# Linear attention and a gated MoE block on one core: MoE chunks of 384 tokens, queries in token order, and TensorE's order fixed as traced

## The chip, the core and the metric

The kernel runs on one core of one Trainium2 chip. The metric is device time in microseconds (us), as the median of several runs. The engines are TensorE (PE; its weight loads are listed as PEld), VectorE (DVE), ScalarE (ACT), GpSimd (POOL) and SyncE (SP), which issues all the DMAs of data here.

## The reference

```python
def _attn_ref(q, k, v, w_phi):                  # q, k, v: 8 batches, 8 heads, 576 tokens, 64
    def phi(x):
        proj = np.einsum('bhsd,df->bhsf', x, w_phi)               # 128 features
        proj = proj - np.max(np.abs(proj), axis=-1, keepdims=True)
        return np.concatenate([np.exp(proj), np.exp(-proj)], axis=-1)
    q_p, k_p = (phi(q), phi(k))
    kv = np.einsum('bhsf,bhsd->bhfd', k_p, v)
    z = np.sum(k_p, axis=2)
    num = np.einsum('bhsf,bhfd->bhsd', q_p, kv)
    den = np.einsum('bhsf,bhf->bhs', q_p, z)[..., None] + 1e-06
    return num / den

def _moe_ref(x, w_in, conv_w, w_out):           # x: 8 x 576 x 512, the heads side by side
    h = np.maximum(x @ w_in, 0.0)               # 1024 wide
    conv_out = sum over k of conv_w[k] * h shifted by k - 1 tokens    # zeros outside a batch
    gate = 1.0 / (1.0 + np.exp(-conv_out))
    return h * gate @ w_out                     # 512 wide
```

## The kernel before

**Attention.** The eight heads of a batch go as two quads (`qd`), and a quad's tokens as five groups (`g`): group 0 is the last 64 tokens of two head pairs, groups 1 to 4 are 256 columns each, two pieces (`t`) of 128 tokens for two heads (`i`). For a group of keys `k_process` loads it, splits it on GpSimd into a high and a low part (`kxh`, `kxl`), multiplies by the feature weights on TensorE in three matmuls a piece (`kp`, L194 to L196), takes the largest absolute value on VectorE (`km`, L199), subtracts it (`ks`, L201), forms both exponentials on ScalarE (`ke`, L223 and L224) and accumulates the product with `v`, which carries a column of ones, in PSUM (`kv`, L236 and L240). When a quad's five groups are done, ScalarE copies the sums out (`kvf`). For a group of queries `q_process` does the same up to `qs`, transposes on TensorE (`tp`, L280), exponentiates (`qe`), multiplies by `kvf` (`nm`, L297) and divides on VectorE (`dn`, `rc`, `x`). Queries of batch 0 are projected without the split, in F32 (L191). `x_process` transposes the result back (`xt`, `xr`) and splits it into `xh` and `xl`, one pair of tiles for a quad of a batch.

**MoE.** A batch's 576 tokens go as two chunks of `TC = 288`, each with one or two columns of its neighbour, 290 in all. `h_part(n)` makes eight tiles of hidden features with 12 matmuls each (`hp`, L356: high by high, low by high, high by low, over four pieces of the 512 inputs), and ScalarE applies the ReLU (`h`). `conv_process(n)` takes the middle tap on GpSimd and the outer taps on VectorE (`c`, L384), one sigmoid over the whole chunk on ScalarE (L388), the gate's product on VectorE (L392) and the split into `gh` and `gl`. `o_part(n)` makes four output tiles with 24 matmuls each (`op`, L415), which ScalarE copies (`os`) and SP writes out. The order is `h_part(n)`, then `o_part(n - 1)`.

**Weights.** `w_in` and `w_out` come as 64-bit floats in 16 tiles. For each, `float64_round` runs four VectorE instructions on a tile `w_t` (L91, L93, L95, L98), two on ScalarE (L92, L97) and one on GpSimd (L100); ScalarE and GpSimd then split it. Two buffers each hold the raw and the rounded tile.

**What sets the order.** All of this is written as generators. A loop at the end (`step`, `runnable`) keeps its own clock `now`, and picks the next step of attention or of the MoE so that the shares left of both shrink alike. A step ends with a cost, for instance `yield pe(450)` for the four (in the trace eight) instructions of a product piece, or with a wait:

```python
        yield pe(330 * n)
        yield wait(3000)
        yield until(back("kv", 1))
```

Chains are begun in the order of the list `chains`: a group of queries, then a group of the next quad's keys. The instructions are then ordered on each engine by a scheduler that plays them through with its own costs; a step runs under `tc.high_priority(offset=...)`, so that attention goes ahead of the MoE there.

Of the kernel before, what the change touches and what calls it, by code (L numbers as in the profile page):

```python
# [20 lines left out]
TC = 288  # L21
HW = TC + 2
VW = D + 1
NH = 11

WINDOW = 13
LAT = 1.7
TAIL_US = 24
AHEAD = 300

NQ_F32 = 2


@with_exitstack
def kernel(
# [108 lines left out]

    now = [0.0]
    ready = {}

    def pe(ns):
        return ("pe", ns)
# [17 lines left out]
    def load_split(src, b, qd, g, kind):  # L167
        c0, n = group_columns(g)
        if kind == "q" and 2 * b + qd < NQ_F32:
            raw = sb.tile([P, n * P], F32, name=f"{kind}r{b}_{qd}_{g}", tag=kind + "xh", bufs=2)  # L170
            nc.sync.dma_start(out=raw, in_=src[b, qd, :, c0 : c0 + n * P])
            return n, raw, None
        raw = sb.tile([P, n * P], F32, name=f"{kind}r{b}_{qd}_{g}", tag=kind + "r", bufs=2)
        nc.sync.dma_start(out=raw, in_=src[b, qd, :, c0 : c0 + n * P])
        hi = sb.tile([P, n * P], F32R, name=f"{kind}xh{b}_{qd}_{g}", tag=kind + "xh", bufs=2)
        lo = sb.tile([P, n * P], F32R, name=f"{kind}xl{b}_{qd}_{g}", tag=kind + "xl", bufs=2)
        split(raw, hi, lo, nc.gpsimd, nc.gpsimd)
        return n, hi, lo

    def project(n, hi, lo, b, qd, g, kind):  # L180
# [6 lines left out]
        for t in range(n):  # L187
            o = ps[:, t * 256 : (t + 1) * 256]
            his = hi[:, t * P : (t + 1) * P]
            if lo is None:  # L190
                nc.tensor.matmul(out=o, lhsT=his, rhs=wbd_f, start=True, stop=True)  # L191
                continue
# [3 lines left out]
            nc.tensor.matmul(out=o, lhsT=los, rhs=wbd_hi, start=False, stop=True)  # L196
        ps3 = ps.rearrange("p (t f) -> p t f", f=F)
        m = sb.tile([P, 2 * n], F32, name=f"{kind}m{b}_{qd}_{g}", tag="m", bufs=4)
        nc.vector.tensor_reduce(out=m, in_=ps3, axis=AX, op=ALU.max, apply_absolute_value=True)  # L199
        pr = sb.tile([P, 2 * n, F], F32, name=f"{kind}s{b}_{qd}_{g}", tag=kind + "s", bufs=2)  # L200
        nc.vector.tensor_tensor(out=pr, in0=ps3, in1=m.unsqueeze(2).broadcast_to([P, 2 * n, F]), op=ALU.subtract)  # L201
# [5 lines left out]
    def k_process(b, qd, g):  # L207
# [4 lines left out]

        yield until(back("kp", 2), back("kv", 4))
        n, hi, lo = load_split(kT, b, qd, g, "k")
        v0 = 16 if g == 0 else 4 * (g - 1)
        v = sb.tile([P, 4 * VW], F32, name=f"v{b}_{qd}_{g}", tag="v", bufs=4)
        nc.sync.dma_start(out=v, in_=vt[b, qd, :, v0 * VW : (v0 + 4) * VW])
# [3 lines left out]
        pr = project(n, hi, lo, b, qd, g, "k")  # L221
        e = sb.tile([P, 2, 2 * n, F], F32, name=f"ke{b}_{qd}_{g}", tag="ke", bufs=2)
        nc.scalar.activation(out=e[:, 0], in_=pr, func=AF.Exp)  # L223
        nc.scalar.activation(out=e[:, 1], in_=pr, func=AF.Exp, scale=-1.0)  # L224
        yield pe(330 * n)
# [5 lines left out]
        for t in range(n):  # L231
            for i in range(2):
                for s in range(2):
                    lhsT = e[:, s, 2 * t + i, :]
                    if g == 0:
                        nc.tensor.matmul(out=kp[i][:, s, :], lhsT=lhsT, rhs=v[:, 2 * i * VW : 2 * (i + 1) * VW],  # L236
                                         start=(s == 0), stop=False, skip_group_check=True)
                    else:
# [4 lines left out]
            yield pe(900 if g == 0 else 450)  # L243
        if g == 4:

            u = 2 * b + qd
            yield until(("num", u - 2, 4) if u > 1 else None)
            r = []
            for i in range(2):
                kf = sb.tile([P, 2, 2 * VW], F32, name=f"kvf{b}_{qd}_{i}", tag="kvf", bufs=4)  # L250
                nc.scalar.activation(out=kf, in_=kp[i], func=AF.Copy)
                r.append(kf)
            kv[b, qd] = r
            set_ready(("kvq", b, qd), 1500)
# [5 lines left out]
    def q_process(b, qd, g):  # L260
        j = (b * NQ + qd) * 5 + g

        def back(key, k):
            return (key, *divmod(j - k, 5)) if j >= k else None

        yield until(back("qp", 2))
        n, hi, lo = load_split(qT, b, qd, g, "q")
        yield wait(3000)
        yield until(back("tp", 2))
        set_ready(("qp", *divmod(j, 5)))  # L270
        pr = project(n, hi, lo, b, qd, g, "q")
        yield pe(330 * n)
        yield wait(1700)
        yield until(back("num", 2))
        set_ready(("tp", *divmod(j, 5)))
# [5 lines left out]
        qe = sb.tile([P, 2, 2, n, P], F32, name=f"qe{b}_{qd}_{g}", tag="qe", bufs=2)  # L281
        for s in range(2):
            nc.scalar.activation(out=qe[:, s], in_=tp, func=AF.Exp, scale=1.0 - 2.0 * s)  # L283
        yield pe(220 * n)
        yield wait(2000)
        yield until(back("num", 1), ("kvq", b, qd))
        if b > 1:
            yield until(("xt", b - 2, qd))
# [5 lines left out]
        for t in range(n):  # L294
# [5 lines left out]
            yield pe(900 if g == 0 else 450)  # L300
        dn = sb.tile([P, n, 2], F32, name=f"dn{b}_{qd}_{g}", tag="dn", bufs=4)
        rc = sb.tile([P, n, 2], F32, name=f"rc{b}_{qd}_{g}", tag="rc", bufs=4)
        x = sb.tile([P, n, 2, D], F32, name=f"x{b}_{qd}_{g}", tag="x0" if g == 0 else "x", bufs=2 if g == 0 else 4)
        xs[b, qd, g] = x
        parts = [(0, 64, 0), (64, 128, VW)] if g == 0 else [(0, P, 0)]
        for a, z, c0 in parts:
            nc.vector.tensor_scalar(out=dn[a:z], in0=ps[a:z, :, :, c0 + D], scalar1=1e-6, scalar2=None, op0=ALU.add)
        nc.vector.reciprocal(out=rc, in_=dn)
        for a, z, c0 in parts:
            nc.vector.tensor_tensor(out=x[a:z], in0=ps[a:z, :, :, c0 : c0 + D],  # L310
                                    in1=rc[a:z].unsqueeze(3).broadcast_to([z - a, n, 2, D]), op=ALU.mult)
        set_ready(("num", *divmod(j, 5)))
        if g == 2 or g == 4:
            spawn(x_process(b, qd, g // 2 - 1))

    def x_process(b, qd, pr):

        yield ("wait", 2500)
        if pr == 0:

            yield until(("h", 2 * (b - 2) + 1) if b > 1 else None)
            xh[b, qd] = sb.tile([P, 2, S], F32R, name=f"xh{b}_{qd}", tag="xh", bufs=4)
            xl[b, qd] = sb.tile([P, 2, S], F32R, name=f"xl{b}_{qd}", tag="xl", bufs=4)
        hi, lo = xh[b, qd], xl[b, qd]
        with tc.high_priority():
            xt = pg.tile([P, 4, P], F32, name=f"xt{b}_{qd}_{pr}", tag="g", bufs=4)
            for t in range(4):
                nc.tensor.transpose(out=xt[:, t, :], in_=xs[b, qd, 1 + 2 * pr + t // 2][:, t % 2], identity=idn)  # L328
            split(xt.rearrange("p t s -> p (t s)"), hi[:, pr, : 4 * P], lo[:, pr, : 4 * P], nc.scalar, nc.vector)
            if pr == 0:  # L330
                xr = pg.tile([P, 2, 64], F32, name=f"xr{b}_{qd}", tag="g", bufs=4)
                nc.tensor.transpose(out=xr, in_=xs[b, qd, 0][:, 0], identity=idn)
                split(xr, hi[:, :, 4 * P :], lo[:, :, 4 * P :], nc.scalar, nc.vector)
        set_ready(("x", b, 2 * qd + pr), 2500)
        if pr == 1:
            set_ready(("xt", b, qd))
        yield pe(550)
# [6 lines left out]
    def h_part(n):  # L344
        b, c = divmod(n, 2)
# [139 lines left out]
    while moe is not None or chains or active:  # L485
# [16 lines left out]
        if can_a and (a_first or not can_m):  # L502
# [3 lines left out]
            if not more:  # L506
                active.remove(p)
# [62 lines left out]
```

## Time and profile before

| | us |
|---|---|
| median of 3 runs | 867.71 |
| lowest and highest | 866.76, 872.09 |
| the profiled execution | 865.62 |
| its span, first to last instruction | 863.8 |

A busy time is the time in which an engine has at least one instruction running. Matmuls overlap: the next one starts while the last one drains, so the duration of one (about 300 ns for the MoE's) says less than the distance between two. The chain of waits, followed back from the last instruction, gives that distance, as it counts for each instruction only what it adds to the chain. Names are those of the program, without the buffer's number: `nm<-kvf,qe` writes `nm` and reads `kvf` and `qe`.

### The profile page before, as it was taken

Reading aid. Unit: us, or ns where it says so; the run is one execution under the profiler, and the core shown is the slowest. Engines: PE = TensorE matmul, PEld = TensorE weight load, DVE = VectorE, ACT = ScalarE, POOL = GpSimd, SP = SyncE. Lnnn points to the kernel's source line nnn. Section 1 sums busy time; section 2 is a strip of 40 time slices with the busy share of each in tenths; the row PEclk is TensorE's granted clock in tenths of the full one; section 3 lists DMA queues with packets and bytes.
Section 4 is the critical chain, followed back from the end, with each engine's and each line's share of the span. In section 5 each row is a group of like instructions: output and inputs, shape, how many; then the busy total and the mean of one; then the engine's idle time right before and its main releaser. Section 6 shows DMA issues by size and latency. Waiting matters only on the chain.

```text
span 863.8 us, 17401 instructions
## 1 busy us (share of the span) xinstructions
PE 832.9 (96%) x6654; PEld 823.9 (95%) x6654; DVE 554.4 (64%) x1222; ACT 401.3 (46%) x812; POOL 279.0 (32%) x466
## 2 busy tenths in 40 slices
PE   7888899999999999999999999999999999999998
PEld 6878899999999998999989999899999999999998
DVE  5999967866657556575566656666566756655461
ACT  4666634745354534435344444444454444433332
POOL 4766844323314132241323314232232412201110
PEclk9998999999999999999999999999999999999999
DMA  6544311112111111211112011211111100000001
GB/s 184 176 144 135 106 49 56 41 37 62 39 58 51 40 44 38 64 45 48 38 52 69 27 53 37 60 56 32 52 50 59 54 27 28 1 28 29 22 14 49
DMA packets 46594, 48.70 MB, mean 56 GB/s; under 512 B 5296, under 2 KB 44464, under 8 KB 46512
## 3 DMA queue, kind: packets, MB, share of 16 engines
q1 hardware_dynamic: 46512, 47.59, 18.3%
q8 instruction: 53, 0.87, 0.4%
q14 instruction: 29, 0.24, 0.1%
HBM read 38.13 MB, written 9.44 MB: 55 GB/s over the span
## 4 chain that ended last, share of the span: by engine, by line
PE 79%; DVE 12%; ACT 4%; issue 2%; DMA 1%; POOL 1%; SPq 0%; ACTq 0%; POOLq 0%; DVEq 0%
PE hp L356 23%; PE op L415 20%; PE nm L297 11%; PE kv L240 9%; PE tp L280 3%; DVE c L392 3%; PE kp L194 2%; PE kp L196 2%; PE qp L194 2%; PE kp L195 2%; PE qp L196 2%; PE qp L195 2%; DVE ks L201 1%; PE xt L328 1%; ACT c L388 1%
## 5 line engine op out<-in xcount | busy, mean ns | idle before, releaser
L384 DVE SCALAR_TENSOR_TENSOR c<-h,cw,c 128x288 f32<-128x288 f32 (+1 forms) x256 | 135.8, 537 | 84.1 <-POOL c L379 80.6
L297 PE MATMUL nm<-kvf,qe 128*128 128x65 f32 (+1 forms) x1152 | 162.7, 268 | 2.5 <-DVE ks L201 1.3
L356 PE MATMUL hp<-xh,win_hi 128*128 128x290 f32 x512 | 155.5, 305 | 0.9 <-ACT os L420 0.7
L297 PEld LDWEIGHTS nm<-kvf,qe 128*128 128x128 f32 x1152 | 152.6, 193 | 3.2 <-issue 1.5
L415 PE MATMUL op<-gh,wout_hi 128*128 128x288 f32 x512 | 154.9, 303 | 0.0
L356 PE MATMUL hp<-xh,win_lo 128*128 128x290 f32 x512 | 154.1, 301 | 0.0
L356 PE MATMUL hp<-xl,win_hi 128*128 128x290 f32 x512 | 153.7, 300 | 0.0
L415 PE MATMUL op<-gl,wout_hi 128*128 128x288 f32 x512 | 153.4, 300 | 0.0
L415 PE MATMUL op<-gh,wout_lo 128*128 128x288 f32 x512 | 152.4, 298 | 0.0
L240 PE MATMUL kv<-v,ke 128*128 128x65 f32 x1024 | 139.8, 267 | 4.6 <-ACT ke L223 4.6
L379 POOL TENSOR_SCALAR c<-h,cw 128x288 f32<-128x288 f32 x128 | 67.1, 525 | 234.7 <-ACT h L363 221.7
L240 PEld LDWEIGHTS kv<-v,ke 128*128 128x128 f32 x1024 | 133.7, 193 | 6.1 <-ACT ke L223 5.9
L363 ACT ACTIVATE h<-hp 128x290 f32<-128x290 f32 x128 | 52.8, 413 | 172.0 <-PE hp L356 164.5
L283 ACT ACTIVATE qe<-tp 128x512 f32<-128x512 f32 (+1 forms) x160 | 79.0, 554 | 49.1 <-PE tp L280 45.1
L356 PEld LDWEIGHTS hp<-xh,win_hi 128*128 128x128 f32 x512 | 96.8, 190 | 1.8 <-ACT os L420 1.4
L356 PEld LDWEIGHTS hp<-xl,win_hi 128*128 128x128 f32 x512 | 97.3, 190 | 0.0
L356 PEld LDWEIGHTS hp<-xh,win_lo 128*128 128x128 f32 x512 | 97.2, 190 | 0.0
L415 PEld LDWEIGHTS op<-gh,wout_lo 128*128 128x128 f32 x512 | 96.4, 188 | 0.0
L415 PEld LDWEIGHTS op<-gl,wout_hi 128*128 128x128 f32 x512 | 96.3, 188 | 0.0
L415 PEld LDWEIGHTS op<-gh,wout_hi 128*128 128x128 f32 x512 | 96.2, 188 | 0.0
L61 POOL TENSOR_SCALAR kxh<-kr 128x256 fp32r<-128x256 f32 (+1 forms) x80 | 33.8, 424 | 192.8 <-PE kp L195 167.8
L392 DVE TENSOR_TENSOR c<-c,h 128x288 f32<-128x288 f32 x128 | 58.4, 526 | 32.7 <-ACT c L388 32.7
(71 smaller groups left out, 1491.2 us busy)
## 6 DMA issues: line engine op xcount, KB each, us to landing
v<-in_vt_dram SPq DMA_DIRECT2D x80, 130.0 KB, 2.1
out_dram<-os SPq DMA_DIRECT2D x64, 144.0 KB, 1.7
qr<-in_qT_dram SPq DMA_DIRECT2D x64, 128.0 KB, 2.1
kr<-in_kT_dram SPq DMA_DIRECT2D x64, 128.0 KB, 2.1
w_r<-in_w_in_dram SPq DMA_DIRECT2D x8, 512.0 KB, 3.4
w_r<-in_w_out_dram SPq DMA_DIRECT2D x8, 512.0 KB, 3.3
qr<-in_qT_dram SPq DMA_DIRECT2D x16, 64.0 KB, 1.9
kr<-in_kT_dram SPq DMA_DIRECT2D x16, 64.0 KB, 2.0
```

The lines of the kernel that those rows point to most:

```text
L194: nc.tensor.matmul(out=o, lhsT=his, rhs=wbd_hi, start=True, stop=False)
L195: nc.tensor.matmul(out=o, lhsT=his, rhs=wbd_lo, start=False, stop=False)
L196: nc.tensor.matmul(out=o, lhsT=los, rhs=wbd_hi, start=False, stop=True)
L240: nc.tensor.matmul(out=kp[i][:, s, p0 : p0 + VW], lhsT=lhsT, rhs=v[:, (2 * t + i) * VW : (2 * t + i + 1) * VW], start=False, stop=(g % 2 = ...
L283: nc.scalar.activation(out=qe[:, s], in_=tp, func=AF.Exp, scale=1.0 - 2.0 * s)
L297: nc.tensor.matmul(out=ps[:, t, i, :], lhsT=qe[:, s, i, t, :], rhs=kv[b, qd][i][:, s, p0 * VW : p0 * VW + w], start=(s == 0), stop=(s == 1))
L356: nc.tensor.matmul(out=ps, lhsT=w_, rhs=x_, start=(k == 0), stop=(k == 11))
L363: nc.scalar.activation(out=hs, in_=ps, func=AF.Relu)
L379: nc.gpsimd.tensor_scalar(out=cv, in0=hs[:, o : o + TC], scalar1=cw[:, f, 1:2], scalar2=0.0, op0=ALU.mult, op1=ALU.add)
L384: nc.vector.scalar_tensor_tensor(out=cv[:, lo:hi], in0=hs[:, o + j - 1 + lo : o + j - 1 + hi], scalar=cw[:, f, j : j + 1], in1=cv[:, lo:hi ...
L392: nc.vector.tensor_tensor(out=c4[:, f, :], in0=c4[:, f, :], in1=hs[:, o : o + TC], op=ALU.mult)
L415: nc.tensor.matmul(out=ps, lhsT=w_, rhs=x_, start=(k == 0), stop=(k == 23))
```

## The change

- The MoE's chunks hold 384 tokens, three for two batches, with 386 columns; the middle chunk of the three crosses the batches' border. There are 12 chunks instead of 16, so 2304 matmuls instead of 3072.
- The queries of a batch go in token order over both quads (`QORDER`), and the list `chains` begins with the keys of both quads of batch 0. Keys run a batch ahead of the queries.
- `x_process(n)` fills a chunk's `xh` and `xl` from sixteen kept tiles `x`. A piece of 128 tokens that lies wholly in the PSUM tile is a transpose; one column at a chunk's border is an ordinary matmul.
- A step of the loop is now as small as one product (two trace instructions) or one MoE matmul, and each has a number of instructions and a time; a list `PACE` says how many MoE instructions may stand beside how many of attention.
- TensorE's order is that of the loop (`manual_schedule`), and the scheduler orders the other engines only. Priority is given to attention's instructions off TensorE (`lead()`), and no longer to the weight tiles.
- The split into `gh` and `gl` is done for two tiles at a time; taps at a batch's border are cut in two; query and key loads share their buffers.

TensorE in the middle of the MoE, at the hidden tiles of the fourth chunk (`hp3`) and attention of batches 3 and 2, before:

```order
L356 MATMUL hp3_3_2693<-xh1_1_2208,win_hi2_93 128x290
L356 MATMUL hp3_3_2693<-xl1_1_2209,win_hi2_93 128x290
L280 MATMUL tp3_0_0_3643<-idn_76,qs3_0_0_3576 128x128
L328 MATMUL xt2_1_1_3649<-idn_76,x2_1_3_3548 128x128 x2
L328 MATMUL xt2_1_1_3649<-idn_76,x2_1_4_3589 128x128 x2
L240 MATMUL kv3_0_0_3374<-v3_0_4_3474,ke3_0_4_3567 128x65
L280 MATMUL tp3_0_0_3643<-idn_76,qs3_0_0_3576 128x128
L240 MATMUL kv3_0_0_3374<-v3_0_4_3474,ke3_0_4_3567 128x65 x3
L240 MATMUL kv3_0_1_3375<-v3_0_4_3474,ke3_0_4_3567 128x65 x4
L356 MATMUL hp3_3_2693<-xh1_1_2208,win_lo2_97 128x290
```

The same engine at the third chunk's outputs (`op2`) and products of batch 4, now:

```order
L258 MATMUL kv4_0_0_3637<-v4_0_2_3724,ke4_0_2_0_3810 128x65
L467 MATMUL op2_0_3803<-gh2_4_3458,wout_hi7_106 128x384
L258 MATMUL kv4_0_0_3637<-v4_0_2_3724,ke4_0_2_1_3812 128x65
L467 MATMUL op2_0_3803<-gl2_4_3459,wout_hi7_106 128x384
L467 MATMUL op2_0_3803<-gh2_4_3458,wout_lo7_114 128x384
L258 MATMUL kv4_0_1_3638<-v4_0_2_3724,ke4_0_2_0_3810 128x65
L467 MATMUL op2_1_3888<-gh2_0_3452,wout_hi0_99 128x384
L258 MATMUL kv4_0_1_3638<-v4_0_2_3724,ke4_0_2_1_3812 128x65
L467 MATMUL op2_1_3888<-gl2_0_3453,wout_hi0_99 128x384
```

Where eight products stood between two MoE matmuls, each product now stands by itself between them.

VectorE near the start, at the last key group of batch 0's second quad (`ks0_1_4`; `w4_t` is the fifth weight tile), before:

```order
L98 SCALAR_TENSOR_TENSOR w4_t_331<-w4_t_331,w4_r_329 128x512
L307 TENSOR_SCALAR dn0_0_1_520<-nm0_0_1_511 128x4
L308 RECIPROCAL rc0_0_1_521<-dn0_0_1_520 128x4
L310 TENSOR_TENSOR x0_0_1_522<-nm0_0_1_511,rc0_0_1_521 128x256
...
L199 TENSOR_REDUCE km0_1_4_658<-kp0_1_4_651 128x4
...
L201 TENSOR_TENSOR ks0_1_4_660<-kp0_1_4_651,km0_1_4_658 128x512
L91 TENSOR_SCALAR w5_t_373<-w5_r_371 128x512
```

At the same key group now (`w14_t` is the fifteenth tile):

```order
L101 TENSOR_SCALAR w14_t_785<-w14_r_783 128x512
L103 TENSOR_SCALAR w14_t_785<-w14_r_783 128x512
L105 SCALAR_TENSOR_TENSOR w14_t_785<-w14_r_783,w14_t_785 128x512
L214 TENSOR_REDUCE km0_1_4_675<-kp0_1_4_668 128x4
L108 SCALAR_TENSOR_TENSOR w14_t_785<-w14_t_785,w14_r_783 128x512
L214 TENSOR_REDUCE km1_0_0_687<-kp1_0_0_683 128x2
L216 TENSOR_TENSOR ks0_1_4_677<-kp0_1_4_668,km0_1_4_675 128x512
```

Five weight tiles stood ahead of this group on VectorE, and now fifteen do.

The diff, cut:

```diff
-TC = 288
+TC = 384
 HW = TC + 2
+HSTART = (0, 383, 766)
+NCH = 12
-NH = 11
+QORDER = [(qd, g + 2 * pr) for g in (1, 2) for qd in range(2) for pr in range(2)] + [(0, 0), (1, 0)]
+NH = 10
+NX = 16
+ISSUE = 112
-TAIL_US = 24
+PACE = ((750, 0), (3300, 1632), (3600, 2016))
+def PE_ORDER(tc):
+    return tc.manual_schedule(engines={mybir.EngineType.PE})
...
-    def pe(ns):
-        return ("pe", ns)
+    def pe(n, ns):
+        return ("pe", n, ns)
...
-        yield until(back("kp", 2), back("kv", 4))
-        n, hi, lo = load_split(kT, b, qd, g, "k")
+        yield until(back("kp", 2), back("kv", 3))
+        with lead():
+            n, hi, lo = load_split(kT, b, qd, g, "k")
...
                         nc.tensor.matmul(out=kp[i][:, s, p0 : p0 + VW], lhsT=lhsT,
                                          rhs=v[:, (2 * t + i) * VW : (2 * t + i + 1) * VW],
                                          start=False, stop=(g % 2 == 0 and t == 1), skip_group_check=True)
-            yield pe(900 if g == 0 else 450)
+                        yield pe(2, 112)
...
     def q_process(b, qd, g):
-        j = (b * NQ + qd) * 5 + g
+        j = 10 * b + QORDER.index((qd, g))
...
-            yield pe(900 if g == 0 else 450)
+                    yield pe(2, 220 if g == 0 else 112)
...
+    def x_process(n):
...
+            for (b, t, a, w, col), q in sorted(zip(tiles, src), key=lambda x: (x[0][1] < 4, x[0][4])):
+                i = (pr * 64 if t == 4 else 0) + a
+                x = xs[q][:, 0 if t == 4 else t % 2]
+                if first + col - i >= 0 and first + col - i + P <= 512:
+                    nc.tensor.transpose(out=xt[:, first + col - i : first + col - i + P], in_=x, identity=idn)
+                    yield pe(1, 60)
+                else:
+                    nc.tensor.matmul(out=xt[:, first + col : first + col + w], lhsT=x, rhs=idn[:, i : i + w], start=True, stop=True)
+                    yield pe(2, 112)
...
                 for w_, x_ in ((wa, xa), (wa, xb), (wb, xa)):
-                    nc.tensor.matmul(out=ps, lhsT=w_, rhs=x_, start=(k == 0), stop=(k == 11))
+                    nc.tensor.matmul(out=ps, lhsT=w_, rhs=x_[:, p, :], start=(k == 0), stop=(k == 11))
                     k += 1
-                if p % 2 == 1:
-                    yield pe(740)
+                    yield pe(1, 173)
...
-    chains = [(0, 0, g, "k") for g in range(5)]
-    for u in range(NQ * B):
-        for g in range(5):
-            chains.append((*divmod(u, NQ), g, "q"))
-            if u + 1 < NQ * B:
-                chains.append((*divmod(u + 1, NQ), g, "k"))
+    chains = [(0, qd, g, "k") for qd in range(NQ) for g in range(5)]
+    for b in range(B):
+        for i in range(10):
+            chains.append((b, *QORDER[i], "q"))
+            if b + 1 < B:
+                chains.append((b + 1, *divmod(i, 5), "k"))
...
+    def paced():
+        for (a0, m0), (a1, m1) in zip(PACE, PACE[1:]):
+            if done["a"] < a1:
+                return m0 + (done["a"] - a0) * (m1 - m0) / (a1 - a0)
+        return 1 << 30
...
             if what == "pe":
-                now[0] += arg
-                left[kind] -= arg
+                n, ns = arg
+                issued[0] = max(issued[0] + ISSUE * n, now[0] - 30 * ISSUE)
+                now[0] = max(now[0], issued[0]) + ns
+                done[kind] += n
...
-        a_first = not start or left["a"] * max(1, start["m"] - TAIL) >= (left["m"] - TAIL) * start["a"]
+            a_first = done["m"] >= paced()
...
-            with tc.high_priority(offset=p[3]):
-                more = step(p, "a")
+                ahead[0] = p[3]
...
+    with PE_ORDER(tc):
+        merge()
```

More of the change, by code (lines that the diff above doesn't have):

```diff
@@ L220, in k_process @@
         set_ready(("kp", j))
[L221 to L225, printed above, removed]
+        pr = yield from project(n, hi, lo, b, qd, g, "k")
+        with lead():
+            e = []
+            for s in range(2):
+                e.append(sb.tile([P, 2 * n, F], F32, name=f"ke{b}_{qd}_{g}_{s}", tag="ke", bufs=3))
+                nc.scalar.activation(out=e[s], in_=pr, func=AF.Exp, scale=1.0 - 2.0 * s)
         yield wait(3000)
@@ L308, in q_process @@
[L308 to L337, printed above, removed]
```

240 lines of the change are left out of this document (146 added, 94 removed).

## The prediction

> **What bounds the kernel now.** I read the page first (shares, slices, chain), then the busy time by stage, then the chain in order of time.
>
> ```profile
> span 863.8 us, 17401 instructions
> PE 832.9 (96%) x6654; PEld 823.9 (95%) x6654; DVE 554.4 (64%) x1222; ACT 401.3 (46%) x812; POOL 279.0 (32%) x466
> PE   7888899999999999999999999999999999999998
> DVE  5999967866657556575566656666566756655461
> PE 79%; DVE 12%; ACT 4%; issue 2%; DMA 1%; POOL 1%; SPq 0%; ACTq 0%; POOLq 0%; DVEq 0%
> ```
>
> TensorE bounds from the sixth slice on. In slices two to five it is VectorE, which stands at 9 there. The stages (columns: length, then busy time and instructions of PE, PEld, DVE, ACT, POOL, granted clock, DMA) say it more sharply:
>
> ```profile
> 0.00:10.00 10.00, 4.98 (x17) 4.06 (x17) 2.54 (x7) 2.00 (x3) 3.03 (x11) 1.00 0.62 170
> ...
> 20.00:40.00 20.00, 16.26 (x125) 15.81 (x125) 18.59 (x33) 12.30 (x24) 15.86 (x17) 0.91 0.50 157
> ...
> 80.00:100.00 20.00, 16.12 (x113) 15.12 (x112) 19.27 (x36) 11.35 (x23) 17.04 (x19) 0.83 0.44 137
> ...
> 110.00:130.00 20.00, 20.00 (x160) 20.00 (x159) 12.07 (x29) 8.26 (x19) 8.49 (x17) 0.91 0.15 41
> ...
> 150.00:760.00 610.00, 602.32 (x4924) 599.30 (x4923) 382.86 (x868) 284.71 (x573) 174.27 (x320) 1.00 0.15 45
> ```
>
> VectorE is full until about 109 us, where the last transposes that waited for it start:
>
> ```profile
> 108.91 0.30 PE L280 MATMUL tp<-idn,qs 128*128 128x128 f32 x1 [1.37 <-DVE qs L201]
> ```
>
> What fills it beside attention is the splitting of the 16 weight tiles, four instructions a tile:
>
> ```profile
> L95 DVE SCALAR_TENSOR_TENSOR w_t<-w_r,w_t 128x512 int32<-128x512 int32 x16 | 15.3, 954 | 0.0
> L98 DVE SCALAR_TENSOR_TENSOR w_t<-w_t,w_r 128x512 f32<-128x512 int32 x16 | 15.2, 947 | 0.0
> L93 DVE TENSOR_SCALAR w_t<-w_r 128x512 int32<-128x512 int32 x16 | 11.4, 713 | 1.6 <-ACT w_t L92 1.5
> L91 DVE TENSOR_SCALAR w_t<-w_r 128x512 int32<-128x512 int32 x16 | 10.3, 648 | 1.6 <-DMA w_r<-in_w_in_dram 1.3 <-POOL win_lo L64 0.3
> ```
>
> A tile is 0.954 + 0.947 + 0.713 + 0.648 = 3.26 us.
>
> **TensorE's prices.** Pieces of the chain (start, length, what) give the cost of one instruction in a run of its kind:
>
> ```profile
> 297.01 4.13 PE op L415 x31
> ...
> 302.36 0.44 PE tp L280 x4
> ```
> ```profile
> 755.91 3.52 PE nm L297 x32
> ...
> 782.55 12.81 PE op L415 x96
> ...
> 834.73 25.59 PE op L415 x192
> ```
> ```profile
> 144.25 0.12 PE kp L196
> ```
> ```profile
> 56.27 1.10 PE L191 MATMUL qp<-wbd_f,qr 128*128 128x256 f32 x4 [0.45 <-PE kp L196]
> ```
>
> MoE 12.81/96 = 0.1334 us; attention's product 3.52/32 = 0.110, I take 0.1115, which the pairs below want; transpose 0.109 from 0.44/4; projection 0.118; F32 projection about 0.22 (1.10 for four, less the last one's drain). A product with F32 operands is two instructions in the trace, so the numerator's 576 are x1152. Now the pattern that the change makes everywhere, which stands in a few places already:
>
> ```profile
> 722.24 0.17 PE kv L240 x2
> 722.41 0.19 PE op L415
> 722.60 0.11 PE tp L280
> 722.71 0.17 PE kv L240 x2
> 722.88 0.19 PE op L415
> 723.07 0.17 PE kv L240 x2
> 723.24 0.12 PE tp L280
> 723.35 0.13 PE op L415
> ```
> ```profile
> 226.51 0.38 PE L415 MATMUL op<-gh,wout_hi 128*128 128x288 f32 x1
> 226.73 0.33 PE L297 MATMUL nm<-kvf,qe 128*128 128x65 f32 x2
> 226.87 0.38 PE L415 MATMUL op<-gl,wout_hi 128*128 128x288 f32 x1
> ...
> 227.22 0.38 PE L415 MATMUL op<-gh,wout_lo 128*128 128x288 f32 x1
> ```
>
> Behind a MoE matmul the pair is cheaper (0.17, not 0.223), but the MoE matmul behind the pair is dearer by as much (0.19, not 0.133). Sum 0.36; the starts at 226.51, 226.87 and 227.22 lie 0.36 and 0.35 apart; apart they cost 0.133 + 2 x 0.1115 = 0.356. Mixing saves nothing. The reading that fits: a weight load starts when the matmul before it starts, not sooner, and lasts some 0.111 us, so a short matmul (0.057) always shows 0.054 of the next load. Only in front of a transpose is that less (0.12 at 723.24, not 0.163), and there the load itself is shorter:
>
> ```profile
> L297 PEld LDWEIGHTS nm<-kvf,qe 128*128 128x128 f32 x1152 | 152.6, 193 | 3.2 <-issue 1.5 <-PE kp L196 1.1 <-ACT qe L283 0.5
> ...
> L328 PEld LDWEIGHTS xt<-idn,x 128*128 128x128 f32 x128 | 15.1, 142 | 2.7 <-issue 1.5 <-PE tp L280 1.1
> ```
>
> 193 less 142 is 51 ns, the 0.048 that such a place saves.
>
> **The change: TensorE's work.** Before: 3072 MoE x 0.1334 + 2304 products x 0.1115 + 810 projections x 0.118 + 36 F32 ones x 0.22 + 432 transposes x 0.109 = 409.8 + 256.9 + 95.6 + 7.9 + 47.1, less 83 products directly in front of a transpose x 0.048 = 813.3 us (counts from the order). After:
> - MoE: 2304 matmuls of 384 or 386 columns. The trace has two widths: 256 (0.118) and 288 (0.1334), 0.461 and 0.463 ns a column, so time goes with the columns: 385 x 0.46 = 0.177, sum 407.8, 2 us less. The other end is a fixed share of some 13 ns a matmul, which these two prices, good to a few ns, can't exclude: 0.1733, 399.3. I take the first, to which both rows point.
> - Transposes: 480 x 0.109 = 52.3. The 16 one-column transposes at chunk borders are F32 matmuls of two instructions; not in the trace, bounded by a transpose below (0.109) and a product above (0.1115): 32 x 0.1115 = 3.6, and 16 MoE loads bared behind them, 1.3.
> - Products before a transpose: 18, so 0.9 saved.
> - Products, projections: same counts, 256.9 + 95.6 + 7.9.
>
> Sum 824.5: 11.2 more than before. [...]
>
> **The start.** The changed program starts with batch 0's keys of both head quads, and TensorE's order is fixed: what stands behind a waiting product waits with it. The first product that uses quad 1's last key group (row 140, `kv0_1_0` from `ke0_1_4`) has only 160 products, 57 projections, 24 F32 projections and 16 transposes ahead: 17.8 + 6.7 + 5.3 + 1.7 = 31.5 us. But it waits through ScalarE's exp for VectorE's row 105, and ahead of that stand 15 weight tiles (5 before), 48.9 us, beside 14 full and 3 small reductions with 16 subtractions (0.68 and 0.41 us each)
>
> ```profile
> L199 DVE TENSOR_REDUCE km<-kp 128x4 f32<-128x512 f32 x64 | 43.5, 682 | 12.6 <-PE kp L196 12.3
> ```
>
> 21.2, two outputs' divisions 1.5 and the first conversions 1.8: 73.4. Of these VectorE does 2.5 in the first 10 us, as before. At the 0.96 busy of 20 to 100 us, with its instructions overlapping a little, the rest needs 68 to 74: 78 to 84. In six tiles L103 now follows L101 at once and must wait for ScalarE between them (0.7 us), and GpSimd needs a tile's buffer back: I take 86. The ends are 78 (no such wait) and 99, where the fifteenth tile of before ended:
>
> ```profile
> 97.84 1.21 DVE L98 SCALAR_TENSOR_TENSOR w_t<-w_t,w_r 128x512 f32<-128x512 int32 x1
> ```
>
> With the exp 0.7 more: TensorE stands at 31.5 us of its work at 86.7, 55 lost. Before, the waiting transpose at 108.9 has 77.6 us of work ahead by the same prices, 31 lost. Nothing later binds harder: the first chunk's last split is only 26 us further down VectorE's list (99.7), while TensorE has 50 us of attention to do before that chunk. The weight tiles' DMAs move up on SP's queue with their splits, and on GpSimd the tiles' products stand between key splits; both queues have room (DMA busy 0.44 to 0.50 and GpSimd 16 of 20 us in the rows above), so I price them within the ends.
>
> **Sum.** Before, from 108.9: 813.3 - 77.6 = 735.7 of work ends at 844.6; TensorE in fact ends at 834.73 + 25.59 = 860.3, so about 15 go to single waits, and 3.5 to the last output. After: 86.7 + (824.5 - 31.5) + 6 + 3.5 = 889. For the single waits I take 6 of 2 to 20, since the order is paced evenly and VectorE, 63% busy between 150 and 760, is ahead there. The profiled execution took 865.62 for its 863.8, so **891 us**; that execution lies 0.2% below the median of 867.71, within the runs' spread.
>
> What else moves hides: conv tap, gate and split on 384 columns are fewer and longer on VectorE, ScalarE and GpSimd (63, 47 and 29% busy between 150 and 760); uncovered they would cost nothing until one fills. The outputs stay at 64 DMAs, since 16 of the 48 tiles cross a batch border and are written in two pieces. Ten buffers for h instead of eleven make a chunk's third ReLU wait for the first gate of the chunk before, and three buffers shared by query and key loads replace two of each: both are asked for long before use, a whole output pass (96 x 0.177 = 17 us) in the one case and 5 us of traced lead in the other; uncovered, either would be a wait at each chunk or group like those of the third rival.
>
> **Rivals.**
> - *Within 1%, about 871*: the start is fast (78.4 + 0.7), MoE has a fixed share (816.0 in all), 2 us of waits: 79.1 + 784.5 + 2 + 3.5 + 1.8. For it: both sizes are inside their bounds. Against: both ends at once. 18%.
> - *Faster, about 853*: behind MoE matmuls that last 0.177, loads get ahead, and a MoE matmul with its pair costs three loads, 0.335 instead of 0.400. Some 586 such pairs stand alone between MoE matmuls: 38 us less; with loads far ahead it would be more. It decides if more than one load can be ready. Against: after 40 MoE matmuls the four transposes at 302.36 still take 0.11 each, and the 32 products at 755.91 pay 0.110 from the start; a pair costs 0.36 with its MoE matmul where three loads would be 0.334. [...] 7%.
> - *Over 913*: the fixed order stalls at each chunk. The sigmoid is one ScalarE instruction over a chunk, 2.13 us now and by elements 2.84 then (estimate from its row), and a ReLU behind it holds one of two PSUM banks; 2 us at each of 12 chunks would be 24. Against: a bank of mixed work lasts 12 x 0.177 and several pairs, over 3 us. 9%.
>
> ```profile
> L388 ACT ACTIVATE c<-c 128x2304 f32<-128x2304 f32 x16 | 34.1, 2129 | 8.7 <-DVE c L384 8.6
> ```
>
> **Numbers.** Three runs spread by 0.6%, so 1% (859.0 to 876.4) is what can be told from no change. The forecast's own case, 876 to 913, has 66%; with the stalls' 9% slower is 75%, same 18%, faster 7%. The range 865 to 913 leaves out the stalls, the faster rival and a little of the same: 80%.
>
> **What would show it.** Right: VectorE at 9 and TensorE well below in the first 85 us; `kv` waiting for `ke` of batch 0 for tens of us around 40 to 86; MoE runs at about 0.177; a pair between MoE matmuls costing 0.40 with its MoE matmul. Wrong: that sum near 0.335; MoE runs at 0.173; VectorE past row 105 at 70 or at 100; many waits of over 0.5 us after 110.

## The result, and the profile after

The changed kernel took **916.29 us** as the median of 4 runs (914.46 to 917.55), the kernel before 867.62 (866.76 to 872.09, 4 runs) beside it: ratio 1.0547, 95% interval 1.0520 to 1.0574. The profiled execution took 917.55 us, its span 915.5. The forecast was 891, with a range of 865 to 913: the sign was right, the time lies just above the range.

The page of the changed kernel, with the slices of TensorE, VectorE and the granted clock:

```profile
span 915.5 us, 15650 instructions
PE 864.3 (94%) x5966; PEld 848.0 (93%) x5966; DVE 544.0 (59%) x1110; ACT 392.3 (43%) x678; POOL 275.8 (30%) x434
PE   5855999999899999999899999999999989999998
DVE  5788654777456575565555556555655545565541
PEclk8565899999899999999999999999999989999999
```

In the first four slices (92 us) TensorE is busy for 5 to 8 tenths, *and* from the second on its clock is granted to little more than a half. VectorE, which stood at 9 there before, no longer does. The stages (columns as in the prediction: length, busy time and instructions of PE, PEld, DVE, ACT, POOL, granted clock, DMA):

```profile
20.00:40.00 20.00, 14.86 (x64) 13.61 (x65) 12.19 (x21) 10.56 (x18) 13.87 (x14) 0.59 0.39 116
...
80.00:100.00 20.00, 14.76 (x74) 14.44 (x75) 14.27 (x21) 9.40 (x18) 14.95 (x14) 0.54 0.29 86
...
150.00:760.00 610.00, 597.86 (x4279) 590.55 (x4278) 360.03 (x753) 262.98 (x456) 178.30 (x302) 0.99 0.16 46
```

Between 20 and 40 us TensorE ran 64 instructions where before it ran 125, VectorE was busy 12.19 us of 20 where it was 18.59, and the clock was 0.59 where it was 0.91.

What TensorE waited for (columns: instruction that waited, what it waited for, us in total, times, longest):

```profile
PE kv L258 <- ACT ke L242: 19.0, 8, 5.2
PE tp L298 <- DVE qs L216: 10.5, 6, 5.3
...
PE xt L375 <- DVE xl L74: 3.6, 1, 3.6
PE nm L321 <- ACT qe L303: 3.5, 3, 1.8
```

Of the first two lines, 18.3 and 6.0 us lie in the first 110 us. The MoE's own matmuls (`hp`, `op`) do not appear in the list. Three waits behind 110 us stand out, in the order of time on TensorE:

```profile
232.66 0.47 PE L375 MATMUL xt<-idn,x 128*128 128x128 f32 x1 [3.56 <-DVE xl L74]
232.78 0.67 PE L467 MATMUL op<-gh,wout_lo 128*128 128x384 f32 x1
...
238.34 0.33 PE L467 MATMUL op<-gl,wout_hi 128*128 128x384 f32 x1
...
439.42 1.38 PE L321 MATMUL nm<-kvf,qe 128*128 128x130 f32 x5 [1.77 <-ACT qe L303]
...
748.95 0.41 PE L298 MATMUL tp<-idn,qs 128*128 128x128 f32 x2 [3.28 <-DVE qs L216]
```

The first of them shows the price of such a wait. TensorE stands for 3.56 us at a transpose `xt`, while the next MoE matmul behind it (`op`) has had its inputs all along. Then, until about 238 us, every MoE matmul lasts 0.67 us instead of 0.33: half pace. The granted clock (the third figure from the end) is 0.50 there and 1.00 on both sides:

```profile
227.91:231.32 3.41, 1.19 (x9) 0.87 (x7) 3.41 (x6) 0.73 (x2) 1.39 (x2) 1.00 0.02 5
231.32:238.15 6.83, 5.49 (x22) 4.97 (x23) 4.50 (x9) 3.16 (x5) 0.00 (x0) 0.50 0.14 48
238.15:241.56 3.41, 3.41 (x24) 3.41 (x23) 2.04 (x4) 2.14 (x5) 2.25 (x4) 1.00 0.14 38
```

To compare kernels I add up, over all matmuls, by how much the distance between the ends of two neighbours exceeds the price of such a pair at full clock (MoE 0.1763 for 386 and 0.1748 for 384 columns, about 0.134 for the shorter ones; the other prices as in the prediction). This sum is called the **loss** below; what is left is TensorE's **work**. **Idle** is the part of the loss in which no matmul was in flight; the rest is half pace, and a little is the first matmul behind a wait (the transpose at 108.91 in the kernel before lasts 0.30 us where the price is 0.109). All in us, split at 110 us:

| kernel | time | work | loss to 110 (idle) | loss behind 110 (idle) |
|---|---|---|---|---|
| before | 867.6 | 813.6 | 26.6 (14.6) | 14.8 (8.3) |
| changed | 916.3 | 820.4 | 59.2 (29.2) | 28.2 (14.9) |

The spans differ by 51.7: 6.8 of work, 32.6 of loss ahead of 110 us and 13.4 behind it, less 1.1 since the first matmul ends earlier. In these two kernels the loss is about twice the idle time, on either side of 110 us.

### The profile page after: what moved, and what is told of

It is laid out like the page before. It is cut to its first block, busy times and chain, and to the rows that moved or that the text cites. A ratio compares the mean times of both kernels' runs of the same rounds, so it can differ in the third digit from the quotient of the medians.

```text
span 915.5 us, 15650 instructions
## 1 busy us (share of the span) xinstructions
PE 864.3 (94%) x5966; PEld 848.0 (93%) x5966; DVE 544.0 (59%) x1110; ACT 392.3 (43%) x678; POOL 275.8 (30%) x434
## 5 line engine op out<-in xcount | busy, mean ns | idle before, releaser
L433 DVE SCALAR_TENSOR_TENSOR c<-h,cw,c 128x384 f32<-128x384 f32 (+3 forms) x256 | 133.1, 546 | 108.7 <-POOL c L427 107.0
L258 PEld LDWEIGHTS kv<-v,ke 128*128 128x128 f32 x1024 | 166.1, 206 | 22.3 <-ACT ke L242 22.0
L406 PE MATMUL hp<-xl,win_hi 128*128 128x386 f32 x384 | 144.1, 375 | 0.0
L406 PE MATMUL hp<-xh,win_hi 128*128 128x386 f32 x384 | 143.5, 374 | 0.0
L406 PE MATMUL hp<-xh,win_lo 128*128 128x386 f32 x384 | 142.0, 370 | 0.0
L467 PE MATMUL op<-gh,wout_lo 128*128 128x384 f32 x384 | 141.5, 368 | 0.0
L467 PE MATMUL op<-gh,wout_hi 128*128 128x384 f32 x384 | 141.1, 367 | 0.0
L467 PE MATMUL op<-gl,wout_hi 128*128 128x384 f32 x384 | 140.0, 365 | 0.1
L427 POOL TENSOR_SCALAR c<-h,cw 128x384 f32<-128x384 f32 x96 | 57.3, 597 | 243.6 <-ACT h L412 242.5
L242 ACT ACTIVATE ke<-ks 128x512 f32<-128x512 f32 (+1 forms) x160 | 88.1, 584 | 93.9 <-DVE ks L216 76.9
L214 DVE TENSOR_REDUCE km<-kp 128x4 f32<-128x512 f32 (+1 forms) x80 | 50.6, 632 | 49.3 <-PE kp L209 49.1
```

The costliest lines, as they stand in the source:

```text
L242: nc.scalar.activation(out=e[s], in_=pr, func=AF.Exp, scale=1.0 - 2.0 * s)
L258: nc.tensor.matmul(out=kp[i][:, s, p0 : p0 + VW], lhsT=lhsT, rhs=v[:, (2 * t + i) * VW : (2 * t + i + 1) * VW], start=False, stop=(g % 2 = ...
L406: nc.tensor.matmul(out=ps, lhsT=w_, rhs=x_[:, p, :], start=(k == 0), stop=(k == 11))
L427: nc.gpsimd.tensor_scalar(out=cv, in0=hs[:, o : o + TC], scalar1=cw[:, f, 1:2], scalar2=0.0, op0=ALU.mult, op1=ALU.add)
L433: nc.vector.scalar_tensor_tensor(out=cv[:, lo:hi], in0=hs[:, o + j - 1 + lo : o + j - 1 + hi], scalar=cw[:, f, j : j + 1], in1=cv[:, lo:hi ...
L467: nc.tensor.matmul(out=ps, lhsT=w_, rhs=x_, start=(i == 0), stop=(i == 23))
```

## The experiments

Twelve kernels ran, all with 4 to 10 runs beside the kernel before. Times are medians. The theory was that the fixed order lets TensorE stand behind a wait while other work is ready; the rivals are named in each expectation.

**1. The fixed order alone.**

```diff
 def PE_ORDER(tc):
-    return tc.manual_schedule(engines={mybir.EngineType.PE})
+    return ExitStack()
```

> The changed kernel with TensorE's order left to the scheduler again; chunks, chains, trace and priorities stay. By the gaps between matmul ends in the changed kernel's trace, its 49 us over before are about 32 of waits ahead of 110 us (59 against 27), 13 of later waits (28 against 15) and 7 of work (820.4 against 813.6). Theory (the fixed order makes a wait of one chain a wait of TensorE): both kinds of wait fall to about before's, 27 to 40 and 10 to 15, and the time to 875 to 895. Rival (chunks of 384 and the new chain list delay what TensorE needs, whatever its order): 905 to 920, with the wait at 91 us still there.

Measured: **863.31 us**, ratio 0.9952 (0.9929 to 0.9976). Work 819.3, loss 22.5 (idle 6.1) ahead of 110 us and 11.8 (7.1) behind it. Both kinds of wait fell, further than expected, and the kernel is slightly faster (0.5%) than the one before. The order by itself costs 916.3 - 863.3 = 53 us, more than the whole 49 by which the change is slower. Its page and a stage of its start:

```profile
PE 840.9 (98%) x5966; PEld 831.7 (97%) x5966; DVE 546.3 (63%) x1110; ACT 388.5 (45%) x678; POOL 277.3 (32%) x434
```
```profile
20.00:40.00 20.00, 18.09 (x120) 17.47 (x119) 16.42 (x33) 12.18 (x23) 11.66 (x13) 0.83 0.54 159
```

120 instructions of TensorE instead of 64 between 20 and 40 us, with the same tiles to round on VectorE. What the scheduler did differently stands in TensorE's rows behind the first key groups. Its order has the projections of the third group and the first of the fourth (`kp0_0_2`, `kp0_0_3`) ahead of the second group's products, which read `ke0_0_1`:

```
L207 MATMUL kp0_0_2_254<-wbd_hi_72,kxh0_0_2_188 128x256
...
L207 MATMUL kp0_0_3_315<-wbd_hi_72,kxh0_0_3_271 128x256
...
L258 MATMUL kv0_0_0_228<-v0_0_1_141,ke0_0_1_0_182 128x65
```

and the order as traced has the whole second group's products ahead of the third group's projection:

```
L258 MATMUL kv0_0_1_231<-v0_0_1_143,ke0_0_1_1_186 128x65
L207 MATMUL kp0_0_2_256<-wbd_hi_72,kxh0_0_2_190 128x256
```

As traced, the projections of the next group or two stand on TensorE behind the products of the group before; these products wait for ScalarE's exponential, that for VectorE's subtraction, and that for the projection: a relay, in which each engine waits for the other in turn. That the order costs the time is measured; that it does so by this relay is a reading of the two orders. Both kernels are built with one order of TensorE's instructions; they differ in who chose it. The scheduler plays all engines through. The loop's clock knows the other engines only as constant latencies.

**2. Mixing single products with MoE matmuls.**

```diff
                         nc.tensor.matmul(out=kp[i][:, s, p0 : p0 + VW], lhsT=lhsT,
...
-                        yield pe(2, 112)
+            yield pe(8, 880 if g == 0 else 448)
```

The step of `nm` was changed in the same way.

> The changed kernel, order still fixed, but a step is again a whole piece (four products of keys or queries in a row), so that no pair of product instructions stands alone between two MoE matmuls (586 do in the changed kernel). Theory (a load starts only with the matmul before it, so mixing hides nothing): TensorE's work stays within 2 us of 820, and the time within 10 us of 916 (the rest is room for other waits). Rival (mixing does hide loads, 65 ns a pair): 38 us more, about 954.

Measured: 926.79 us, ratio 1.0680 (1.0629 to 1.0731). Work 820.7 against 820.4: the theory's value, and none of the 38 us of the rival. The time is just over the 10 us allowed, by waits: loss 59.2 (28.5) and 35.6 (18.9).

**3. The kernel before, with its order fixed.** The loop at its end was put under the same `manual_schedule`, with nothing else changed.

> The kernel before with nothing changed but that TensorE's order is fixed as traced. Theory (a fixed order stands behind every wait that the tracing clock did not foresee): 10 to 40 us slower than 867.6, most of it ahead of 110 us, where VectorE splits the weight tiles. Rival (the fixed order costs only with the new chain list and the large chunks): 865 to 875.

Measured: **983.48 us**, ratio 1.1343 (1.1314 to 1.1372), far beyond the theory's 10 to 40. Work 816.2, loss 50.3 (25.1) and 106.0 (61.3). So the fixed order costs 116 us with the old trace, and 53 with the new one. It does not need the new chain list or the large chunks. What TensorE waits for there:

```profile
PE qp L194 <- DVE ks L201: 24.4, 5, 5.8
PE tp L280 <- DVE qs L201: 18.5, 12, 2.6
```

**4. The order fixed from the first MoE matmul on.**

```diff
-    with PE_ORDER(tc):
-        merge()
+    merge(lambda: done["m"] == 0)
+    with PE_ORDER(tc):
+        merge(lambda: True)
```

(`merge` runs its loop while the argument holds.)

> The changed kernel with the order free until the first MoE matmul and fixed from there on. It splits the two kinds of wait. Theory: the waits ahead of 110 us fall from 59 to about 30 and the later ones stay near 28, so 885 to 892. Rival (chain list and weight tiles make the start, not the order): 905 to 920, with the start as in the changed kernel.

Measured: 887.85 us, ratio 1.0229 (1.0194 to 1.0265); loss 28.4 (11.6) and 30.1 (15.7). As the theory had it: the start's loss falls by 31 us, the later one stays.

**5. The gate's product moved off VectorE.**

```diff
-            nc.vector.tensor_tensor(out=c4[:, f, :], in0=c4[:, f, :], in1=hs[:, o : o + TC], op=ALU.mult)
+            nc.gpsimd.tensor_tensor(out=c4[:, f, :], in0=c4[:, f, :], in1=hs[:, o : o + TC], op=ALU.mult)
```

> The changed kernel, order fixed, with the gate's product on GpSimd and no longer on VectorE. In the changed kernel the wait of 3.56 us at 232.7 is that of a transposed chunk's split standing behind seven gate products (4.10 us) on VectorE. Theory (later waits are TensorE standing behind chunk-long blocks of another engine): that wait goes, with the slow stretch behind it (6 us together); the waits at 439 (behind the sigmoid on ScalarE) and 749 (behind the splits) stay: 908 to 913. Rival (something else is always late next): within 2 us of 916.

Measured: 909.56 us, ratio 1.0477 (1.0443 to 1.0510); loss behind 110 us 22.0 (11.5), 6.2 less, as the theory had it. The place on VectorE in the changed kernel, where the two splits stood behind the gates:

```profile
227.91 4.10 DVE L441 TENSOR_TENSOR c<-c,h 128x384 f32<-128x384 f32 x7 [0.96 <-ACT c L437]
232.04 0.56 DVE L74 TENSOR_TENSOR xl<-xt,xh 128x386 fp32r<-128x386 f32 x1
```

The wait at `xt` for `xl` falls from 3.6 to 0.3 us, and the other two stayed (1.77 and 3.28 us, at 432 and 740 us).

**6. Longer latencies in the loop's clock.**

```diff
-LAT = 1.7
+LAT = 3.0
```

> The changed kernel, order fixed, with the tracing clock's latencies between engines taken 3.0 instead of 1.7 times. Theory (a fixed order waits where that clock reckoned too little): the later waits, 28 us behind 110 us, fall to 10 to 20, the 59 ahead of 110 us stay, since nothing but attention can be traced there: 898 to 910. Rival (the order of rows on VectorE and ScalarE makes the waits, not the lead on TensorE): 912 to 925.

Measured: 924.97 us, ratio 1.0640 (1.0593 to 1.0688); loss 55.8 (28.5) and 41.1 (16.3). The theory missed: the later loss rose instead of falling, and the time is the rival's. The larger constant moved the waits; 16.4 us of loss now stand between 150 and 200 us and 10.0 behind 850. So longer constant latencies alone do not cure the waits; only this one value was run. That the loop's clock lacks what stands ahead on the other engine fits with this run and with 5, but no run isolates it.

**7. The start without VectorE's rounding.** `float64_round` kept its ScalarE and GpSimd instructions and lost the four of VectorE.

> The changed kernel, order fixed, with the weights' rounding from 64 bits left out on VectorE (the four instructions a tile; ScalarE, GpSimd and the loads stay, and the weights are not the reference's). Theory (the start's 59 us are the fixed order waiting for VectorE behind the weight tiles): 15 tiles less, 49 us of VectorE, and the waits ahead of 110 us fall to 15 to 30: 872 to 887. Rival (the fixed order waits there for GpSimd's splits and its own chains, with or without the tiles): 900 to 916.

Measured: 896.52 us, ratio 1.0323 (1.0287 to 1.0359), between the theory and the rival, and nearer to the rival. Loss ahead of 110 us about 41 instead of 59.2, idle 14.4 instead of 29.2. Two of its stages:

```profile
20.00:40.00 20.00, 16.31 (x80) 15.36 (x79) 5.58 (x10) 15.67 (x29) 13.80 (x16) 0.59 0.55 159
...
60.00:80.00 20.00, 17.57 (x79) 16.34 (x78) 5.18 (x9) 7.45 (x14) 9.17 (x13) 0.52 0.23 70
```

VectorE is over two thirds idle, and TensorE still waits and still has about half its clock. The product that waits for the last key group starts at 72.75 us (with rounding 91.04; the same row of TensorE's order). The weight tiles are worth 18 us there. With the tiles and a free order (run 1) the loss is 22.5, so most of the rest goes with the order, and with the clock that its waits leave behind.

**8. The clock.** Before the products of each of batch 0's ten key groups TensorE got 20 transposes that nobody needs:

```diff
+        if b == 0:
+            for z in range(20):
+                nc.tensor.transpose(out=kvps[b, qd][0][:, 384:], in_=idn, identity=idn)
```

They write into spare columns of the PSUM tile in which batch 0's sums are open, and the output of this run differs from the reference's by a relative 0.27.

> The changed kernel, order fixed, with 20 idle transposes of the identity (about 2.2 us at 0.109 each) ahead of each of batch 0's ten key groups' products: 22 us more work for TensorE, put where it waits. In the changed kernel's start TensorE has 29 us without a matmul, yet the loss is 59, since matmuls behind a wait run at half pace (granted clock 0.50 to 0.67 between 20 and 100 us). Theory (the waits bring the slow stretches): the granted clock there rises above 0.8, and the time is no longer than the changed kernel's, 900 to 920, in spite of the 22 us. Rival (the clock is low there for another reason): still 0.5 to 0.67, and 925 to 950.

Measured: 912.36 us, ratio 1.0501 (1.0463 to 1.0538), against 1.0547 for the changed kernel: not slower, with 22.3 us more of work (842.7). Loss 30.6 (13.0) ahead of 110 us instead of 59.2 (29.2). The granted clock is above 0.8 in three of the four stages that the theory named. Between 20 and 100 us it was 0.59, 0.67, 0.50 and 0.54, and is now:

```profile
20.00:40.00 20.00, 16.46 (x138) 15.59 (x137) 16.90 (x26) 11.98 (x22) 13.21 (x14) 1.00 0.45 142
40.00:60.00 20.00, 16.92 (x100) 16.02 (x100) 14.76 (x28) 10.90 (x20) 10.52 (x11) 0.74 0.40 127
60.00:80.00 20.00, 17.63 (x126) 17.21 (x125) 12.46 (x20) 8.80 (x15) 11.80 (x13) 0.83 0.45 138
80.00:100.00 20.00, 18.01 (x146) 16.77 (x144) 17.73 (x29) 12.40 (x24) 12.95 (x12) 1.00 0.35 106
```

So the waits bring the low clock: with transposes to do in them, TensorE was granted more.

**9. The chunk's length, with the order fixed and free.** `TC = 288`, 16 chunks, with `HSTART`, the border cases and `PACE` to match.

> The changed kernel, order fixed, with chunks of 288 tokens as before (16 chunks; sigmoid, gate products and splits a quarter shorter). TensorE's work by the prices is 8 us more than with 384 (3072 x 0.1334 + 48 more transposes and 141 more bared pairs). Theory (chunk-long blocks): the waits behind 110 us fall from 28 to 12 to 22, the time 908 to 920. Rival (the chunk's length has no part in the waits): 28 of them stay, 922 to 930.

Measured: 921.00 us, ratio 1.0609 (1.0575 to 1.0644); work 824.9 (4.5 more than with 384, not 8), loss 56.8 (27.0) and 28.9 (18.6). The time lies between the theory and the rival, and the loss is the rival's. As an account of the whole later loss, the theory of chunk-long blocks fell here: a quarter shorter, they leave the same loss behind 110 us, in 8 waits of over 1 us instead of 3. That single waits stand behind such blocks (run 5) is not touched by this.

> The changed kernel with chunks of 288 tokens and TensorE's order left to the scheduler; beside the run with 384 and a free order (863.3 us, work 819.3, waits 34) it shows what the larger chunk is worth by itself. By the prices, 3072 matmuls at 0.1334 against 2304 at 0.1755 are 5.4 us more, 48 more transposes 5 us less hidden, waits the same: 870 to 876. Rival (longer blocks cost as much as the fixed share saves): 860 to 866.

Measured: **863.11 us**, ratio 0.9939 (0.9914 to 0.9965); work 823.6, loss 27.2 (8.8) and 2.9 (1.8). This is the rival's time, and as the rival had it: with 384 tokens TensorE has some 4 us less work, and with 288 it loses some 4 us less in all. That longer blocks are the reason is not shown: 6.8 us of the loss with 384 are the one wait at 800 us and its slow stretch, which an earlier pace also removes (run 10). The large chunk by itself is worth nothing that this comparison can tell.

**10. Free order, paced earlier, and in groups.**

```diff
-PACE = ((750, 0), (3300, 1632), (3600, 2016))
+PACE = ((750, 0), (3300, 1500), (3600, 1800))
```

> The changed kernel with a free order and attention paced earlier (its last instructions beside MoE instruction 1800 instead of 2016). With a free order two waits are left behind 130 us, one of 3.3 us at 800, where the last query group's exponential stands behind two splits and a table load on ScalarE and no MoE work is ready, followed by a slow stretch: 6.8 us together. Theory: with attention done earlier there is MoE work to take, and the time is 855 to 860. Rival (the wait moves to another place): 861 to 866.

Measured: 862.66 us, ratio 0.9932 (0.9904 to 0.9961). The loss behind 110 us is 7.7 (4.3) instead of 11.8 and the wait at 800 us is gone, but the median moved by less than the runs' spread (858.82 to 864.34) and lies in the rival's range. With run 1 and the free order with 288 it is one of three versions that are faster than the kernel before, all by 0.5 to 0.7%.

> The changed kernel with a free order and the products traced a piece at a time (single pairs between MoE matmuls: 14 instead of 314). Theory (mixing neither hides nor costs TensorE anything): 860 to 867, as with the free order alone (863.3). Rival (mixing is worth something once no order is fixed): over 870.

Measured: 868.44 us, ratio 1.0005 (0.9984 to 1.0027), between the two expectations. Work is 819.5, as with single products (819.3), so mixing hides nothing here either; the 5 us are loss, 14.8 (8.6) behind 110 us. That a finer trace gives the scheduler finer steps to choose from would explain this; no run tests it.

## Why the prediction was right and wrong

**TensorE's work: right.** I had 11.2 us more, and the traces have 6.8. Most of the difference is the MoE's price, for which I took 0.177 with 0.1733 as the other end. Two runs of MoE matmuls (first and last of 96 `hp`, first and last of 30 `op`):

```profile
816.83 0.33 PE L406 MATMUL hp<-xh,win_hi 128*128 128x386 f32 x1
...
833.55 0.33 PE L406 MATMUL hp<-xh,win_lo 128*128 128x386 f32 x1
...
835.82 0.33 PE L467 MATMUL op<-gh,wout_hi 128*128 128x384 f32 x1
...
840.84 0.33 PE L467 MATMUL op<-gh,wout_lo 128*128 128x384 f32 x1
```

16.72/95 = 0.176 and 5.02/29 = 0.173; over the whole trace it is 0.1763 and 0.1748, between the two ends. From 288 to 384 columns the price rises by 0.041 (0.1334 to 0.1748), less than the 0.044 that goes with the columns. By these two prices there is a fixed share, but they do not settle its size: worked out from 0.1748 it is about 9 ns, from the 0.173 of the 30 `op` about 14 (both estimates). No run shows the 13 ns behind my 0.1733 by itself; what the runs showed in its place are the prices 0.1763 and 0.1748.

**Mixing saves nothing: right.** A pair with its MoE matmul:

```profile
168.34 0.33 PE L258 MATMUL kv<-v,ke 128*128 128x65 f32 x2
168.48 0.42 PE L406 MATMUL hp<-xh,win_hi 128*128 128x386 f32 x1
168.74 0.33 PE L258 MATMUL kv<-v,ke 128*128 128x65 f32 x2
```

0.40 from pair to pair, as worked out, and not 0.335. Run 2 confirms it on the whole kernel. The faster rival is out: in the trace of neither kernel does a weight load start before the matmul ahead of it has started (6654 loads before, 5966 in the changed kernel; the closest start is 1 ns behind).

**The start: near in number, by luck.** Row 140 was forecast at 86.7 us and came at 91.04:

```profile
85.46 0.41 PE L209 MATMUL kp<-wbd_hi,kxl 128*128 128x256 f32 x1
91.04 1.21 PE L258 MATMUL kv<-v,ke 128*128 128x65 f32 x4 [5.16 <-ACT ke L242]
```

The working took VectorE to be full, 0.96 busy, with 15 weight tiles ahead. It was busy for 12.19, 18.19 and 15.88 us of 20 in the three stages from 20 us on, and it waited itself, as this line of its waits up to 92 us shows:

```profile
DVE w_t L103 <- ACT w_t L102: 10.9, 12, 2.7
```

Without the tiles' VectorE work the row still came at 72.75 (run 7), where the working, less the 48.9 us of the tiles, would have had it at about 38. So the tiles account for 18 of the 49 us put down to them. The rest goes with the traced order (runs 1 and 4: with the same tiles and a free start the loss is that of before) and with a clock that fell to a half (run 8).

**The single waits: the step that failed.** The prediction put "6 of 2 to 20" behind row 140, "since the order is paced evenly and VectorE, 63% busy between 150 and 760, is ahead there". The trace has 31.5. The forecast's sum with what came: 86.7 became 91.0 (+4.3), the 793.0 of work 789 (-4), and the 6 of waits 31.5 (+25.5); the last output's 3.5 stayed. That is the miss. The term fails twice. An even pace on TensorE says nothing of what stands ahead on VectorE or ScalarE at the moment when a product needs them: behind 110 us the idle time alone is 14.9 us, 8.6 of it in the three waits shown. The first stood behind VectorE's gate products (run 5), the second behind a sigmoid and a table load on ScalarE, the third behind two splits and a subtraction of keys on VectorE:

```profile
434.91 2.76 ACT L437 ACTIVATE c<-c 128x3072 f32<-128x3072 f32 x1
437.69 1.28 ACT L303 ACT_TABLE_LOAD   x1
```
```profile
745.85 2.02 DVE L74 TENSOR_TENSOR gl<-c,gh 128x768 fp32r<-128x768 f32 x2
...
748.39 0.41 DVE L216 TENSOR_TENSOR qs<-qp,qm 128x256 f32<-128x256 f32 x1
```

And these three waits are paid about twice, since half pace comes with each (6.83, 3.41 and 6.83 us at a granted clock of 0.50), which the term had at nothing.

**The rivals.** "Over 913" named the time that came (916), and its ground, that the fixed order stalls, is right. Its mechanism is not: no hidden tile waited for a PSUM bank behind the sigmoid; the one wait behind a sigmoid (at 439) is that of attention's exponential. The waits are at `xt`, `nm` and `tp`, at few places and not at each chunk, and chunks of 288 lose as much (run 9). Its 9% was too little for the case that TensorE's order is the matter. "Within 1%" asked for a start at 79.1 and 2 us of waits; what came is 91.0 and 31.5.

**What would show it.** TensorE low in the first 85 us and 0.40 for a pair came. The `kv` waits came with 18.3 us in the first 110, less than "tens". "VectorE at 9" did not come. MoE runs came once by the sign of being right (`hp`, 0.176) and once by that of being wrong (`op`, 0.173). "Many waits of over 0.5 us after 110" did not come either: there are seven, as many as in the kernel before. Few but long waits are what none of these signs asked for.

## What to carry to other kernels

An engine order written by a loop with its own clock is as good as what that clock knows of the other engines; fixed on the busiest engine, it turned a change worth about half a per cent into one that costs 5%, and on the old trace 13%. Before fixing an order, run the same trace with the scheduler's, and look at the first place where the two differ. In a sum, price a wait of TensorE at more than its length (here the loss was 1.6 to 3.7 times the idle time, about twice in the changed kernel), and look at the clock of the stage as well as at who is busy.

## What the runs showed of the hardware

Half pace can follow a wait of 1.80 us. In the kernel with free order and grouped products, TensorE waits that long for an exponential; 2.1 us later the MoE's matmuls are 0.32 us apart, and 3.5 us after that about 0.175 again:

```profile
193.31 2.30 PE L257 MATMUL kv<-v,ke 128*128 128x65 f32 x16 [1.80 <-ACT ke L242]
195.41 0.54 PE L466 MATMUL op<-gl,wout_hi 128*128 128x384 f32 x1
195.74 0.53 PE L466 MATMUL op<-gh,wout_lo 128*128 128x384 f32 x1
...
198.62 0.51 PE L466 MATMUL op<-gh,wout_lo 128*128 128x384 f32 x1
198.94 0.36 PE L466 MATMUL op<-gh,wout_hi 128*128 128x384 f32 x1
199.14 0.33 PE L466 MATMUL op<-gl,wout_hi 128*128 128x384 f32 x1
```

It is not certain for each wait of that length: in run 8 one of 2.19 us, right behind 20 transposes, was not followed by it.

```profile
24.27 2.30 PE L261 MATMUL kv<-v,ke 128*128 128x65 f32 x16 [2.19 <-ACT ke L242]
26.37 0.37 PE L207 MATMUL kp<-wbd_hi,kxh 128*128 128x256 f32 x1
26.57 0.28 PE L208 MATMUL kp<-wbd_lo,kxh 128*128 128x256 f32 x1
```

In the traces of the two kernels the granted clock is 0.50 in ten stretches that lie inside the run: 3.41, 3.41, 6.83 and 3.41 us long before, and 13.65, 17.07, 40.96, 6.83, 3.41 and 6.83 in the changed kernel, so 3.41 us or a whole multiple of it. In the changed kernel the waits of 3.56, 1.77 and 3.28 us come with the last three of these, from 231.32, 439.53 and 750.15 us on. That is 1.3 us before the end of the first wait, 0.1 behind that of the second and 1.2 behind that of the third. In such a stretch a MoE matmul takes 0.32 us (`hp` from 752 to 756 us) instead of about 0.175, which makes these three waits cost about twice their length. Where many shorter waits follow each other, as in the first 110 us, it can be more: 22.5 us of loss for 6.1 idle in run 1, about 41 for 14.4 in run 7.

In run 8 the granted clock rose from 0.59 to 1.00 between 20 and 40 us with nothing but transposes of F32 added on TensorE. Why half pace follows one wait of about 2 us and not another, no run shows.
